# Scores of a pair of heads in two stretches instead of three, with the attention product inside the first

## The chip, the cores and the metric

The kernel runs on one core of a Trainium2 chip. The metric is the device time of one execution in microseconds (us); lower is better. A core has engines that run side by side, each through its own list of instructions in order: TensorE (PE in the profile; its weight loads are PEld), VectorE (DVE), ScalarE (ACT), GpSimd (POOL) and SyncE (SP), which here issues most DMAs. They wait for one another through semaphores. TensorE writes its results to PSUM, which has eight banks of 512 fp32 words per partition; DVE and ACT read them from there.

## The reference

```python
# attention: q, k, v of shape (8, 8, 576, 64), tau = 0.02
scores = scale * np.matmul(q, k.transpose(0, 1, 3, 2))
thresh = np.max(scores, axis=-1, keepdims=True) - tau
scores = np.where(scores >= thresh, scores, -1000000000.0)
scores = scores - np.max(scores, axis=-1, keepdims=True)
attn = np.exp(scores)
attn = attn / (np.sum(attn, axis=-1, keepdims=True) + 1e-09)
attn_out = np.matmul(attn, v)
# bridge: (B, H, S, D) -> (B*S, H*D) = (4608, 512), then the feed-forward block, d_ff = 1536
g = x @ w_gate
silu = g * (1.0 / (1.0 + np.exp(-g)))
out = (silu * (x @ w_val)) @ w_out
```

All is fp32. Each row of scores keeps only what lies within tau of its largest value.

## The kernel before

The eight batches are taken in turn, and in each the eight heads in four pairs. The first four pairs (batch 0) go through an older scheme in the head of the program (up to about 130 us). The other 28 pairs, the "halved" ones, are what the change is about. While their attention runs for batch b, TensorE also computes the feed-forward block of batch b - 1, so that the matmuls of the one fill the time in which the other waits for DVE and ACT. From about 1152 us on, only feed-forward work is left (the tail).

**A pair of heads.** Its 576 queries are cut into nine units of 64. A unit's scores for one head fill 128 partitions x 288 words of PSUM: the partitions hold two groups of 32 queries, each against two halves of the keys. They are made by matmuls on narrow tiles of the array (64 rows x 32 columns), eight of them side by side for two heads. A PSUM bank takes one unit in words 0 to 287; a third unit is laid in the rest of two banks, 144 words in each. So with two banks per head, four in all, a slot of three units (`NU3 = 3`) is computed at once: units 0 and 1 in the banks' first parts, unit 2 in the two halves behind them. A pair has three slots. The other four PSUM banks (`bank0` to `bank3`, handed out by `take`) are for everything else: the attention product and the feed-forward matmuls.

**A slot.** `slot_scores` (L1690) waits until the masks of the slot before have left the banks, takes one tile of two banks per head (`pss`) and issues the matmuls (L1706). `slot_rest` (L1711) then plans, for six score tiles (three units, two heads):

- four reductions on DVE for the negated row maximum (L1727 takes two units of a head, L1729 the third);
- the exchange between the two halves of the keys, on DVE (L1735, L1736) or as four copies on ACT (L1741) and a minimum on DVE (L1745), as `MAX_BY_ACT` says;
- the threshold `th` on ACT (L1748);
- per tile an exponential on ACT (L1752), which reads the scores in PSUM and writes to `pall` in SBUF, and a mask on DVE (L1754), which reads the scores again, zeroes what is below the threshold and sums the row;
- the exchange of the sums on ACT (L1762), total and reciprocal on DVE (L1767, L1768), scaling on ACT (L1780) or POOL (L1777), as `POOLED` says, and a transposition on DVE (L1782).

Which of them waits for which is taken by the framework from the tiles that an instruction reads and writes, in the order in which the program writes the instructions down.

**The attention product** of a pair (`attend`, L1787; matmuls L1803) needs all nine units of it transposed, and takes two of the four general banks. It is issued in the next pair, right ahead of that pair's second slot (L1959), so that product and scores share one visit to the narrow tiles. ACT copies the result to `xall` (L1814, L1815).

**The order.** The program writes its instructions down in an order that a planner works out. A `Job` has an engine, an estimated duration, a rank and its predecessors; `Plan` keeps a clock for each engine and takes the job that can start first, by rank. TensorE's order is fixed by the program: `pe(took, fn, *deps)` first brings all jobs to the clock's time, then writes the matmuls and moves TensorE's clock on. The tables `GV`, `CH`, `CD`, `PLAIN` and `CH0` say how many steps of feed-forward work stand behind each slot. Such a step is one of the seven matmul groups of a `Group` (`pa`, `pb`, `pe`, L994), a nested product of `Deep` (`px`, L1474), a flat one (`py`, L1483), or for the first batches a product of `Outputs` (`po`, L1270) or of a plain group (L1201). A `Group`'s steps wait for copies on ACT (L1001, L1017, L1023, L1038, L1069) and free their banks with DVE (L1047, L1059).

The score matmuls before, and the loop over the slots:

```python
for u, part, keys in ((0, (0, slice(0, SH)), (0, SH)), (1, (1, slice(0, SH)), (0, SH)),
                      (2, (0, slice(SH, SH + SQ)), (0, SQ)), (2, (1, slice(SH, SH + SQ)), (SQ, SH))):
...
for s, (n, x) in enumerate((n, x) for n in range(len(halved)) for x in range(NU3)):
...
    if x == 1 and n > 0:
        prepare_v(seg, attend(halved[n - 1]))
    pss, mark = slot_scores(seg, t)
```

## Time and profile before

| | us |
|---|---|
| runs | 1373.98, 1371.77, 1370.46 |
| median | 1371.77 |
| span of the profiled execution | 1370.5 |

| line | engine, what | times | mean ns |
|---|---|---|---|
| L994 | PE, gate step's matmul, 128x256 | 2496 | 380 to 382 |
| L1706 | PE, score matmul, 288 or 144 wide | 5376 | 345 |
| L1803 | PE, attention product | 4032 | 404 |
| L1752 | ACT, exponential | 504 | 498 |
| L1754 | DVE, mask | 504 | 514 |
| L1727 | DVE, maximum of two units | 168 | 743 |
| L1729 | DVE, maximum of the third unit | 168 | 445 |
| L1762 | ACT, exchange of sums, four to a slot | 336 | 198 |
| L1782 | DVE, transposition | 252 | 765 |
| L1780 | ACT, scaling | 415 | 527 |
| L1777 | POOL, scaling | 89 | 1008 |

The span runs from the first to the last instruction of the profiled execution. Matmuls overlap in the array, so a matmul's duration is not what it costs; the distance from one group's start to the next group's start is. Each fp32 matmul of the program leaves two records in the trace. In a line of the timeline stand the start, the time until the group's last end, engine, line, operation, what is written and read, and how many; a bracket tells how long the engine was idle before and who released it. In the view of waits a line reads: who waited, for whom, then us in total, times, longest.

### The profile page before, as it was taken

What the parts mean: (1) busy time and instruction counts of PE and PEld (TensorE: products, weight loads), DVE (VectorE), ACT (ScalarE), POOL (GpSimd) and SP (SyncE); (2) the same over time, 40 slices, a digit from 0 to 9 for tenths busy, and PEclk for the clock granted to TensorE, in tenths of its full rate; (3) what the DMA queues carried; (4) which work ended last, traced back from release to release, by engine and by line L of the source; (5) the groups of instructions that cost most, each with busy time, mean ns of one, the idle gap of its engine ahead of it and who ended that gap; (6) DMA issues with size and microseconds to landing.
All of it is one profiled execution on the core that took longest, in us unless ns stands there. A gap on an engine that the chain in (4) does not pass through costs nothing.

```text
span 1370.5 us, 39181 instructions
## 1 busy us (share of the span) xinstructions
PE 1352.0 (99%) x15590; PEld 1117.2 (82%) x15590; DVE 1069.8 (78%) x2815; ACT 872.3 (64%) x2261; POOL 717.4 (52%) x665
## 2 busy tenths in 40 slices
PE   8999999999999999999999999999999999999998
PEld 6777787778788788877887888877887788999998
DVE  6788888887877777777778777777777776787786
ACT  6888776666756766676767766776767764330330
POOL 2688598663564669434973387427943593000000
PEclk9999999999999999999999999999999999999999
DMA  8752424545524541554154514553165404524411
GB/s 174 196 191 77 96 60 129 142 122 154 159 52 151 145 99 29 175 165 118 37 169 129 150 36 130 141 145 87 33 195 144 113 19 143 162 77 141 157 64 32
DMA packets 208294, 162.32 MB, mean 118 GB/s; under 512 B 166128, under 2 KB 180464, under 8 KB 202736
## 3 DMA queue, kind: packets, MB, share of 16 engines
q1 hardware_dynamic: 203920, 158.86, 41.1%
q8 instruction: 124, 2.03, 0.7%
q10 hardware_dynamic: 4192, 0.95, 0.3%
q14 instruction: 58, 0.48, 0.1%
HBM read 138.28 MB, written 21.50 MB: 117 GB/s over the span
## 4 chain that ended last, share of the span: by engine, by line
PE 90%; DVE 3%; POOL 2%; SPq 1%; DMA 1%; issue 1%; ACT 1%; ACTq 0%; DVEq 0%; POOLq 0%
PE pb L994 18%; PE pa L994 12%; PE px L1474 12%; PE sc L1706 10%; PE pe L994 9%; PE xa L1803 9%; PE po L1270 5%; PE py L1483 5%; PE sc L1155 2%; PE pg L1201 2%; PE pv L1201 2%; PE pe L1155 1%; SPq L367 1%; POOL big L334 1%; PE sc L1474 1%
## 5 line engine op out<-in xcount | busy, mean ns | idle before, releaser
L1754 DVE SCALAR_TENSOR_TENSOR pall<-sc,th,pall 128x288 f32<-128x288 f32 x504 | 244.0, 514 | 65.6 <-ACT pall L1752 51.2
L994 PE MATMUL pb<-xall,big 128*128 128x256 f32 x1152 | 273.5, 380 | 0.0
L1752 ACT ACTIVATE pall<-sc,nm 128x288 f32<-128x288 f32 x504 | 232.1, 498 | 34.2 <-DVE pall L1754 33.9
L994 PEld LDWEIGHTS pb<-xall,big 128*128 128x128 f32 x1152 | 216.3, 190 | 31.0 <-issue 2.5
L1782 DVE STREAM_TRANSPOSE pall<-pall 128x576 f32<-128x576 f32 x252 | 189.7, 765 | 57.8 <-ACT pall L1780 41.1
L1780 ACT ACTIVATE pall<-pall,ri 128x288 f32<-128x288 f32 x415 | 189.4, 527 | 26.3 <-DVE ri L1768 25.8
L847 POOL TENSOR_TENSOR hall<-hall,tmp 128x512 f32<-128x512 f32 x80 | 102.2, 1277 | 159.0 <-DVE hall L1047 141.6
L994 PE MATMUL pa<-xall,big 128*128 128x256 f32 x768 | 183.4, 382 | 0.0
L994 PEld LDWEIGHTS pa<-xall,big 128*128 128x128 f32 x768 | 143.0, 190 | 22.2 <-issue 2.7
L1706 PE MATMUL sc<-kT,qT 64*32 64x144 f32 (+1 forms) x5376 | 149.7, 345 | 3.0 <-DVE pall L1754 1.7
L1727 DVE TENSOR_REDUCE mx<-sc 128x2 f32<-128x576 f32 x168 | 124.8, 743 | 28.4 <-PE sc L1706 27.9
L1706 PEld LDWEIGHTS sc<-kT,qT 64*32 64x32 f32 x5376 | 98.0, 106 | 56.9 <-issue 21.1
L994 PE MATMUL pe<-xall,big 128*128 128x256 f32 x576 | 137.2, 381 | 0.7 <-issue 0.7
L1803 PE MATMUL xa<-pall,vall 64*32 64x288 f32 x4032 | 132.4, 404 | 0.9 <-DVE hall L1047 0.8
L1777 POOL TENSOR_SCALAR pall<-pall,ri 128x288 f32<-128x288 f32 x89 | 88.7, 1008 | 67.1 <-DVE ri L1768 63.9
L994 PEld LDWEIGHTS pe<-xall,big 128*128 128x128 f32 x576 | 108.5, 190 | 17.5 <-issue 3.0
L1803 PEld LDWEIGHTS xa<-pall,vall 64*32 64x32 f32 x4032 | 76.4, 107 | 50.1 <-issue 7.0
L1762 ACT COPY sums<-sums 32x6 f32<-32x6 f32 x336 | 66.6, 198 | 45.7 <-DVE pall L1754 41.1
L1046 ACT ACTIVATE vall<-tmp 128x512 f32<-128x512 f32 x96 | 60.1, 629 | 24.8 <-POOL tmp L847 9.1
L1483 PE MATMUL py<-wo,hall 128*128 128x256 f32 x336 | 74.8, 379 | 0.0
L1729 DVE TENSOR_REDUCE mx<-sc 128x1 f32<-128x288 f32 x168 | 74.7, 445 | 0.0
L847 POOL TENSOR_TENSOR tmp<-tmp 128x512 f32<-128x512 f32 x36 | 45.8, 1273 | 53.4 <-ACT tmp L1069 53.3
(258 smaller groups left out, 2470.9 us busy)
## 6 DMA issues: line engine op xcount, KB each, us to landing
big<-sums_hbm SPq DMA_DIRECT2D x42, 1024.0 KB, 5.3
big<-sums_hbm SPq DMA_DIRECT2D x48, 768.0 KB, 4.8
vall<-in_v_dram SPq DMA_DIRECT2D x112, 144.0 KB, 3.0
out_dram<-big SPq DMA_DIRECT2D x32, 256.0 KB, 2.9
qT<-in_q_dram SPq DMA_DIRECT2D x112, 72.0 KB, 4.7
kT<-in_k_dram SPq DMA_DIRECT2D x112, 72.0 KB, 3.1
wo<-in_moe_w_gate_dram SPq DMA_DIRECT2D x16, 384.0 KB, 4.5
wo<-in_moe_w_val_dram SPq DMA_DIRECT2D x16, 384.0 KB, 4.6
```

The costliest lines, as they stand in the source:

```text
L847: return lambda: nc.gpsimd.tensor_tensor(out=out, in0=a, in1=b, op=op)
L994: nc.tensor.matmul(ps[:, i], w[:, k_, i * P:(i + 1) * P], x[:, k_, :], start=first and i == k_ == 0, stop=True, skip_group_check=True)
L1474: nc.tensor.matmul(ps, a[:, f, :], ws[n][:, f, :], start=bank_ not in begun, stop=True, skip_group_check=True)
L1483: nc.tensor.matmul(ps(), a[:, f, i * P:(i + 1) * P], operands[o][:, f, :], start=first and f == 0, stop=True, skip_group_check=True)
L1706: nc.tensor.matmul(pss[h][(slice(g * G, (g + 1) * G), *part)], qT[hs, col:col + G], kT[hs, c * SH + keys[0]:c * SH + keys[1]], start=True, ...
L1727: rs.append(job("DVE", 0.72, lambda n=n, tile_=tile_: nc.vector.tensor_reduce(out=mx[:, n:n + 2, 0], in_=tile_[:, :, 0:SH], axis=AX.X, op= ...
L1752: ej = job("ACT", 0.42, lambda x=x, n=n: nc.scalar.activation(ps[x], scs[x], AF.Exp, bias=nm[:, n:n + 1]), ej, *((masks[h, 0], masks[h, 1] ...
L1754: masks[x] = job("DVE", 0.45, lambda x=x, n=n: nc.vector.scalar_tensor_tensor(out=ps[x], in0=scs[x], scalar=th[:, n:n + 1], in1=ps[x], op0 ...
L1777: scaled.append(job("POOL", 1.02, lambda x=x, n=n: nc.gpsimd.tensor_scalar(out=x, in0=x, scalar1=ri[:, n:n + 1], scalar2=None, op0=ALU.mul ...
L1780: scaled.append(job("ACT", 0.46, lambda x=x, n=n: nc.scalar.activation(x, x, AF.Copy, scale=ri[:, n:n + 1]), rj, rank=rank))
L1782: seg["turned"].append(job("DVE", 0.72, lambda both=both: nc.vector.transpose(out=both, in_=both), *scaled, rank=rank))
L1803: nc.tensor.matmul(holds[a].ap()[x * G:(x + 1) * G, 0:SH].rearrange("d (i q) -> d i q", q=G), vr[rs, h, j, ds], p[rs, h, :, j, :], start=( ...
```

## The change

The nine units of a pair are computed in two stretches instead of three slots: a combined one of six units and a plain one of three. In the combined stretch TensorE computes two units (in the banks' first parts, "place 0" and "place 1"), then the attention product of the pair before, then four units: one in the halves behind (`HALVES`), one each in place 0 and place 1 again, and one in two of the general banks (`held`). The first pair keeps three plain stretches.

- The four score banks become one tile, `sc_all`, used throughout; `sc_of` gives each head's half of it, and `sc_users` holds for each place the masks that must have read it.
- `unit_scores` issues one unit; `group_scores` and `group_rest` take the place of `slot_scores` and `slot_rest`, for two, three or four units. Maxima in place 0 or 1 are reduced for both heads of a unit at once, the others head by head. The exchange can be divided between ACT and DVE (`BOTH`).
- The jobs of the first two units go ahead of others (`top=-1`).
- The steps of feed-forward work come from one generator (`sequence`) and new tables (`EARLY`, `SECOND`, `THIRD`, `MAIN`); which scalings go to POOL, who does the exchange, and where weight sums are placed is set anew.
- Smaller ones: `take` may now use the last bank that holds a copied value where it is free 0.8 us sooner; `take_b` and `p1` change which groups copy early; some loads get further predecessors.

```diff
-    ps_s = ctx.enter_context(tc.tile_pool(name="ps_s", bufs=2, space=bass.MemoryType.PSUM))
+    ps_s = ctx.enter_context(tc.tile_pool(name="ps_s", bufs=1, space=bass.MemoryType.PSUM))
...
+    sc_all = ps_s.tile([P, 4, 512], F32, name="sc")
+    sc_of = [sc_all[:, 2 * h:2 * h + 2] for h in range(2)]
...
+    def pieces_of(place, h):
+
+        if place == HALVES:
+            return [(sc_of[h][:, n, SH:SH + SQ], n * SQ, (n + 1) * SQ) for n in range(2)]
+        return [(sc_of[h][:, place, 0:SH] if isinstance(place, int) else place[h].ap()[:, 0:SH], 0, SH)]
...
+    def unit_scores(seg, unit, place, more, *deps):
+
         qT, kT = seg["qT"], seg["kT"]
-        deps, sc_users[:] = sc_users[:], []
-        pss = []
+        held = place if isinstance(place, list) else []
 
         def fn():
-            pss.extend(ps_s.tile([P, 2, 512], F32, name="sc") for _ in heads)
...
+            for pieces in zip(*(pieces_of(place, h) for h in range(2))):
                 for g in range(NG):
                     a, c = divmod(g, 2)
...
+                    for (to, lo, hi), hs in zip(pieces, heads):
+                        col = unit * D + a * G
+                        nc.tensor.matmul(to[g * G:(g + 1) * G], qT[hs, col:col + G], kT[hs, c * SH + lo:c * SH + hi], start=True, stop=True)
+
+        users = [d for x in held for d in x.deps] if held else sc_users.pop(place, [])
+        return pe(UNIT + more, fn, *users, *deps)
...
+        for u in sorted(range(U), key=lambda u: marks[u]):
+            if isinstance(places[u], int):
+                def reduce(u=u):
+                    nc.vector.tensor_reduce(out=both_mx[:, :, u], in_=sc_all[:, places[u]:4:2, 0:SH], axis=AX.X, op=ALU.max, negate=True)
+
+                rs.append(job("DVE", 0.74, reduce, marks[u], rank=top))
+                continue
...
         for h, u in tiles:
             x, n = (h, u), n_of(h, u)
-            ej = job("ACT", 0.42, lambda x=x, n=n: nc.scalar.activation(ps[x], scs[x], AF.Exp, bias=nm[:, n:n + 1]), ej,
-                     *((masks[h, 0], masks[h, 1]) if u == 2 else ()), rank=0)
-            masks[x] = job("DVE", 0.45, lambda x=x, n=n: nc.vector.scalar_tensor_tensor(
+            bank_mates = [masks[h, y] for y in range(U) if (h, y) in masks and HALVES in (places[u], places[y])
+                          and not isinstance(places[y], list) and not isinstance(places[u], list)]
+            ej = job("ACT", 0.44, lambda x=x, n=n: nc.scalar.activation(ps[x], scs[x], AF.Exp, bias=nm[:, n:n + 1]), ej, *bank_mates, rank=top)
+            masks[x] = job("DVE", 0.48, lambda x=x, n=n: nc.vector.scalar_tensor_tensor(
...
+    EARLY = (2, 2, 4, 1, 4, 3, 5, 2, 5)
+    SECOND = (5, 9, 5, 9, 8, 9, 7, 4)
+    THIRD = (5, 9, 6, 8, 10, 7, 2, 3)
+    MAIN = (3, 10, 6, 8, 10, 7, 2, 3)
...
+        if len(units) > 3:
+            marks = group_scores(seg, units[0:2], [0, 1], True, False)
+            group_rest(seg, units[0:2], [0, 1], marks, pooled[0], by[0], 2, top=-1)
             prepare_v(seg, attend(halved[n - 1]))
+            holds = []
+
+            def held():
+                holds.extend(take("sc") for _ in range(2))
+                return holds
+
+            marks = group_scores(seg, units[2:6], [HALVES, 0, 1, held], False, True)
+            group_rest(seg, units[2:6], [HALVES, 0, 1, holds], marks, pooled[1], by[1], 2, BORDER)
+        else:
+            marks = group_scores(seg, units, [0, 1, HALVES], True, True)
```

## The prediction

> **What bounds the kernel now.** First the page's first part, then TensorE's waits.

> ```profile
> span 1370.5 us, 39181 instructions
> PE 1352.0 (99%) x15590; PEld 1117.2 (82%) x15590; DVE 1069.8 (78%) x2815; ACT 872.3 (64%) x2261; POOL 717.4 (52%) x665
> ```
> ```profile
> PE sc L1706 <- DVE pall L1754: 1.7, 2, 1.1
> PE xa L1803 <- DVE hall L1047: 0.8, 5, 0.2
> ```

> TensorE works 99% of the span, and in the attention part its two largest waits are 1.7 and 0.8 us in total. So a microsecond taken from TensorE there counts in full, and so does one that it has to wait. The timeline of TensorE shows what a visit to the scores (L1706) costs:

> ```profile
> 796.43 1.89 PE L994 MATMUL pb<-xall,big 128*128 128x256 f32 x8
> 798.16 1.89 PE L994 MATMUL pa<-xall,big 128*128 128x256 f32 x8
> 799.98 1.72 PE L1706 MATMUL sc<-kT,qT 64*32 64x288 f32 x64
> 801.62 1.99 PE L994 MATMUL pb<-xall,big 128*128 128x256 f32 x8
> 803.45 1.89 PE L994 MATMUL pe<-xall,big 128*128 128x256 f32 x8
> ...
> 783.40 4.60 PE L1803 MATMUL xa<-pall,vall 64*32 64x288 f32 x144
> 787.79 1.70 PE L1706 MATMUL sc<-kT,qT 64*32 64x288 f32 x64
> ```

> A gate step (L994) takes 1.73 us from start to start; before the scores 1.82, after them 1.83. The attention product is 144 records in 4.39 us, eight at a time on the array, so a wave of eight 288-wide ones takes 0.244. A unit is two waves (0.49; one of 144-wide halves is four short waves, the same), three units 1.46, but the visit takes 1.64 inside: a visit costs 0.09 + 0.18 + 0.10 = 0.37 us beside its work.

> Now what hangs on the scores: the reductions (L1727, L1729), the exchange (L1741), the limit (L1748), six exponentials on ACT (L1752), six masks on DVE (L1754), all reading the same PSUM. DVE and ACT in the same slot:

> ```profile
> 801.91 0.72 DVE L1727 TENSOR_REDUCE mx<-sc 128x2 f32<-128x576 f32 x1
> 802.56 0.44 DVE L1729 TENSOR_REDUCE mx<-sc 128x1 f32<-128x288 f32 x1
> ...
> 806.79 0.52 DVE L1754 SCALAR_TENSOR_TENSOR pall<-sc,th,pall 128x288 f32<-128x288 f32 x1 [1.43 <-ACT pall L1752]
> ...
> 807.23 0.52 DVE L1754 SCALAR_TENSOR_TENSOR pall<-sc,th,pall 128x288 f32<-128x288 f32 x1
> ...
> 807.88 0.52 DVE L1754 SCALAR_TENSOR_TENSOR pall<-sc,th,pall 128x288 f32<-128x288 f32 x1
> ```
> ```profile
> 804.06 0.81 ACT L1741 COPY mx<-mx 32x6 f32<-32x6 f32 x4 [0.59 <-DVE mx L1729]
> ...
> 806.06 0.30 ACT L1748 ACTIVATE th<-nm,cut 128x6 f32<-128x6 f32 x1
> 806.27 0.88 ACT L1752 ACTIVATE pall<-sc,nm 128x288 f32<-128x288 f32 x2
> 807.35 0.94 ACT L1752 ACTIVATE pall<-sc,nm 128x288 f32<-128x288 f32 x2 [0.20 <-DVE pall L1754]
> ```

> The third exponential starts at 807.35, 0.04 after the first mask has ended (806.79 + 0.52), though ACT was idle and the two read different banks: accesses of two engines to one PSUM tile go one after the other, in the order written out. Before, each head has its own tile, so the two heads alternate and a mask comes every 0.55 us on average. From these starts: mask to next exponential 0.56, exponential to its mask 0.53.

> **What the change removes.** Visits fall from 85 to 58 (84 score stretches and a last product; now 30 three-unit stretches, 27 combined ones, one product): 27 x 0.37 = 10.0 us gained. The work itself stays: 288-wide score matmuls rise by 216 and 144-wide ones fall by 432, the same time.

> **What it adds: waits in the combined stretch.** All four banks are now one tile (sc_all). In the changed kernel's instruction list each wait names a semaphore's count; in 24 of the 27 combined stretches they read: mask 1 waits for exponential 2, exponential 3 for mask 1, mask 2 for exponential 3, exponential 4 for mask 2, mask 3 for exponential 4; the HALVES unit on TensorE waits for mask 3, mask 4 for HALVES's last matmul, and the unit in place 0 for mask 4. Let T be the first of the two early units' matmuls.
> - Scores end at T + 1.23 (1.72 less two waves). Two reductions of 576: start to start 0.65 (801.91 to 802.56), the last 0.74: T + 2.69 with 0.07 before.
> - Exchange, minimum and limit: 0.81 + 0.13 + 0.2 and hops on ACT, 1.28; on DVE 1.11 (from the slot at 787.79, where reductions end at 791.71 and the first exponential starts at 792.82). First exponential at about T + 3.9.
> - Two exponentials 0.88, then 0.04, 0.56, 0.53, 0.56, 0.53, 0.52 to mask 3's end: T + 7.52; HALVES 0.08 later at T + 7.6.
> - TensorE is there at T + 1.0 + 4.39 = T + 5.39: it waits 2.2. Then HALVES 0.7 with its flight, hop, mask 0.52, hop: place 0 comes 1.35 after HALVES instead of 0.49, another 0.86. Sum 3.07; in the three stretches where both masks precede HALVES, 2.65.
> - 24 x 3.07 + 3 x 2.65 = 81.7 us. Bounds for one stretch: 0.9 if the masks ran at the old pace bank by bank (rival below), 4.0 where the product itself also waits for the last transposes, which now have one stretch less before it. That second wait I worked out for one stretch with eight gate steps before it: transposes and the gate sum end 1.0 to 1.3 late; I take 0.3 on average, 8 us.

> [...]

> **Waits behind it.** The four-unit group's chain is serial too. From place 0: scores of both places end at + 1.2; six reductions 2.8 (four of 0.37 and two of 0.65 apart); exchange and limit 1.25; eight exponentials and masks, of which the shared tile's alternate, end near + 12.4. TensorE has 1.73 and the work up to the next stretch, which by the instruction list and the rows (gate step 1.73, nested product 4.7, flat product 5.2) is 5.2, 10.4, 8.6, 13.8, 18.1, 10.4, 10.3, 17.2 and then, in turn, 9.9, 8.1, 10.3, 17.2 us. Where less than 10.7 there is a wait: 5.5, 0.3, 2.1, 0.3, 0.4 and about 0.8 + 2.6 + 0.4 per block of four pairs. Together some 24 us (0 if gates lag anyway, 40 if foreign instructions stand between). The three-unit chain (+ 11.3) is covered by gaps of 10.3 to 19.3. Gate steps queue behind exponentials on ACT, which is in order: the copies they wait for come 0.4 and 0.2 late in the stretch I walked through, 0.6 in some 13 stretches, 8 us.

> Costed at nothing: 21 scalings move from ACT (0.527) to POOL (1.008), covered by POOL's 48% idle, 21 us if not; loads of q, k and v keep their number and are issued by SP, whose transfers keep 41% of the DMA engines busy; bank choice and late copies add one DVE addition of about 0.7 in all.

> **Sum.** -10.0 + 81.7 + 8 + 24 + 8 = +111.7. 1370.5 + 111.7 = 1482.2 for the span; the median of the runs is 1.3 above the profiled span, so 1483.

> **The rivals.**
> 1. Waits only by bank: the masks keep 0.55 and HALVES waits for its own banks' masks. Mask 4 would end at T + 6.5, HALVES's second half be due at 5.63: 0.9 x 27 = 24, and 5 behind it: 1370.5 - 10 + 24 + 5 + 1.3 = 1391. For it: the earlier kernel waits so little. Against: 807.35, and the waits as listed.
> 2. The other side: faster. By data alone nothing is late: masks 1 and 2 end at T + 5.4 ahead of place 0 at 5.88, mask 4 at 6.5 against place 1 at 6.4. If the product's 4.39 us cover the chain, only the visits count: 1371.8 - 10.0 = 1361.8. It decides if mask 3 ends before T + 5.3; by the rows it does so 2.2 later, and among the 84 stretches of the trace no fourth mask ended sooner than 7.6 after the first score matmul, with one unit more in front.
> 3. The clock drops as TensorE pauses. The granted clock is 0.88 in the first 10 us, where TensorE is busy 6.57, and 1.00 from 785 to 932. If it halved for one visit and one gate step after each combined stretch: 27 x (1.46 + 1.73) = 86 more, 1569. Against: pauses of 2.2 and 0.86 with work between. [...]

> **How the numbers follow.** Forecast 0.83 (own range 1425 to 1525: waits of 2.4 and nothing behind them give 1427, of 4.0 with 45 behind 1515); rival 1 0.06, rival 2 0.07, rival 3 0.04. The range 1385 to 1525 takes in rival 1 and nine tenths of the forecast, 0.81. A measurement of this kernel tells about 0.3% from no change: faster 0.08, same 0.01, slower 0.91.

> **What would show it.** TensorE waiting on the mask line in front of the narrow halves and of place 0, some 2.2 and 0.9 us in each combined stretch, 27 times; exponentials and masks of the early two units in strict turn, 1.1 us a pair; waits on the mask line before three-unit stretches that come 8 to 10 us after a combined one; 58 visits to the narrow tiles. Wrong if HALVES starts right behind the product, or if masks still come every 0.55 us.

## The result and the profile after

The changed kernel takes 1534.58 us (median of 4 runs, 1531.78 to 1539.47) against 1371.12 for the kernel before on the same chip: a ratio of 1.120, with a 95% interval of 1.117 to 1.122. The forecast was 1483 with a range up to 1525: the direction was right, the size too small. The profiled execution has a span of 1529.8 us, 159.3 more than before; the forecast for it was 111.7 more.

From the page of the changed kernel, its first part and two of its costliest groups (busy time and mean ns of one, then the engine's idle time before them and what ended most of it):

```profile
span 1529.8 us, 38164 instructions
...
PE 1379.0 (90%) x15158; PEld 1125.1 (74%) x15158; DVE 1082.3 (71%) x2837; ACT 856.1 (56%) x2214; POOL 744.4 (49%) x691
...
L1806 DVE SCALAR_TENSOR_TENSOR pall<-sc,th,pall 128x288 f32<-128x288 f32 x504 | 248.8, 516 | 206.8 <-ACT pall L1805 180.5
L1805 ACT ACTIVATE pall<-sc,nm 128x288 f32<-128x288 f32 x504 | 230.8, 496 | 117.9 <-DVE pall L1806 114.0
```

The same two groups of the kernel before:

```profile
L1754 DVE SCALAR_TENSOR_TENSOR pall<-sc,th,pall 128x288 f32<-128x288 f32 x504 | 244.0, 514 | 65.6 <-ACT pall L1752 51.2
L1752 ACT ACTIVATE pall<-sc,nm 128x288 f32<-128x288 f32 x504 | 232.1, 498 | 34.2 <-DVE pall L1754 33.9
```

TensorE's share falls from 99% to 90%. A mask still takes 516 ns and an exponential 496; but before its masks DVE now waits 180.5 us for exponentials instead of 51.2, and ACT 114.0 us for masks instead of 33.9. The two engines stand still for one another. TensorE's own waits (for whom, us in total, times, longest):

```profile
PE sc L1732 <- DVE pall L1806: 88.3, 63, 6.3
PE sc L447 <- DVE pall L472: 16.7, 11, 2.5
PE pb L1006 <- ACT tmp L1056: 7.5, 6, 1.4
PE xa L1862 <- DVE pall L1841: 6.1, 5, 2.6
PE pb L1006 <- ACT tmp L1087: 4.7, 13, 0.6
PE sc L453 <- DVE pall L472: 4.2, 4, 1.4
```

Scores waiting for masks: 88.3 us where it was 1.7. The lines L447, L453 and L472 are scores and masks in the head of the program, which the prediction had not looked at. The chain of waits in one combined stretch (start, us, what was being waited out):

```profile
932.61 1.22 PE sc L1732 x32
...
933.85 1.43 DVE mx L1766 x2
...
936.17 0.30 ACT th L1798
...
936.47 0.79 ACT pall L1805 x2
...
937.28 0.54 DVE pall L1806 x2
...
937.84 0.51 ACT pall L1805
...
938.38 0.54 DVE pall L1806 x2
...
938.94 0.51 ACT pall L1805
...
939.47 0.54 DVE pall L1806 x2
...
940.05 0.81 PE sc L1732 x32
...
940.88 0.54 DVE pall L1806 x2
...
941.46 3.07 PE sc L1732 x48
```

This is the prediction's chain almost to the tenth. By the timeline the first of these score matmuls starts at 932.54, so that is the forecast's T. The first exponential starts at T + 3.93 (forecast 3.9), then exponentials and masks come in turn, the halves at T + 7.51 (forecast 7.6), then mask 4, and place 0 comes 1.41 behind the halves (forecast 1.35). The product (by the timeline from 933.53 to 938.1) is not in the chain at all: TensorE then stands still for 1.95 us. What the forecast didn't have is the last line: the 48 matmul records of the last three units in 3.07 us, where the same 48 take 1.69 elsewhere.

By stages, from the spans of four profiled executions (us; "16 pairs" is from the product of the tenth halved pair to that of the 26th; the product stands about a third of a pair earlier in the new order, so some 10 us lie in the last column instead of the second):

| kernel | to the first halved score | to the tenth product | 16 pairs | to the end |
|---|---|---|---|---|
| before | 132.0 | 356.7 | 589.0 | 292.8 |
| changed | 140.8 | 412.0 | 663.6 | 313.3 |
| changed, two tiles (first experiment) | 129.0 | 375.1 | 618.0 | 308.3 |
| before, one tile (second experiment) | 140.7 | 406.2 | 643.2 | 299.2 |

### The profile page after: what moved, and what is told of

It reads as the page before. It is cut to its first block, busy times and chain, and to the rows that moved or that the text cites. A ratio compares the mean times of both kernels' runs of the same rounds, so it can differ in the third digit from the quotient of the medians.

```text
span 1529.8 us, 38164 instructions
## 1 busy us (share of the span) xinstructions
PE 1379.0 (90%) x15158; PEld 1125.1 (74%) x15158; DVE 1082.3 (71%) x2837; ACT 856.1 (56%) x2214; POOL 744.4 (49%) x691
## 3 DMA queue, kind: packets, MB, share of 16 engines
q8 instruction: 120, 1.97, 0.5%
## 4 chain that ended last, share of the span: by engine, by line
PE 41%; DVE 16%; ACT 9%; issue 3%; POOL 1%; DVEq 0%; ACTq 0%; POOLq 0%
PE pb L1006 10%; PE px L1492 8%; PE sc L1732 7%; ACT pall L1805 6%; DVE pall L1806 6%; PE pa L1006 5%; DVE mx L1766 4%; PE py L1501 4%; PE pe L1006 3%; DVE mx L1773 2%; PE sc L1173 1%; DVE pall L1841 1%; ACT mx L1784 1%; PE pe L1173 1%; DVE mx L1779 1%
## 5 line engine op out<-in xcount | busy, mean ns | idle before, releaser
L1806 DVE SCALAR_TENSOR_TENSOR pall<-sc,th,pall 128x288 f32<-128x288 f32 x504 | 248.8, 516 | 206.8 <-ACT pall L1805 180.5
L1805 ACT ACTIVATE pall<-sc,nm 128x288 f32<-128x288 f32 x504 | 230.8, 496 | 117.9 <-DVE pall L1806 114.0
L1006 PE MATMUL pb<-xall,big 128*128 128x256 f32 x1104 | 266.6, 384 | 12.5 <-ACT tmp L1056 7.5
L1006 PEld LDWEIGHTS pb<-xall,big 128*128 128x128 f32 x1104 | 205.9, 191 | 56.2 <-ACT tmp L1056 11.9
L1732 PE MATMUL sc<-kT,qT 64*32 64x288 f32 (+1 forms) x4944 | 164.4, 392 | 88.3 <-DVE pall L1806 88.3
L1836 POOL TENSOR_SCALAR pall<-pall,ri 128x288 f32<-128x288 f32 x110 | 110.5, 1015 | 218.1 <-DVE ri L1827 215.8
L1732 PEld LDWEIGHTS sc<-kT,qT 64*32 64x32 f32 x4944 | 83.5, 112 | 161.2 <-DVE pall L1806 119.8
L1839 ACT ACTIVATE pall<-pall,ri 128x288 f32<-128x288 f32 x394 | 183.1, 527 | 10.1 <-DVE ri L1827 9.2
L1862 PEld LDWEIGHTS xa<-pall,vall 64*32 64x32 f32 x4032 | 99.9, 108 | 38.9 <-DVE tmp L1077 7.2
L1006 PEld LDWEIGHTS pe<-xall,big 128*128 128x128 f32 x576 | 108.6, 190 | 16.6 <-issue 1.4
L1821 ACT COPY sums<-sums 32x4 f32<-32x4 f32 (+2 forms) x336 | 66.7, 199 | 53.3 <-DVE pall L1806 48.9
L1784 ACT COPY mx<-mx 32x6 f32<-32x6 f32 (+2 forms) x162 | 31.7, 196 | 113.7 <-DVE mx L1773 84.6
L1798 ACT ACTIVATE th<-nm,cut 128x6 f32<-128x6 f32 (+2 forms) x84 | 25.0, 297 | 108.6 <-DVE nm L1793 89.7
```

Source lines behind the costliest of these rows:

```text
L1006: nc.tensor.matmul(ps[:, i], w[:, k_, i * P:(i + 1) * P], x[:, k_, :], start=first and i == k_ == 0, stop=True, skip_group_check=True)
L1732: nc.tensor.matmul(to[g * G:(g + 1) * G], qT[hs, col:col + G], kT[hs, c * SH + lo:c * SH + hi], start=True, stop=True)
L1805: ej = job("ACT", 0.44, lambda x=x, n=n: nc.scalar.activation(ps[x], scs[x], AF.Exp, bias=nm[:, n:n + 1]), ej, *bank_mates, rank=top)
L1806: masks[x] = job("DVE", 0.48, lambda x=x, n=n: nc.vector.scalar_tensor_tensor(out=ps[x], in0=scs[x], scalar=th[:, n:n + 1], in1=ps[x], op0 ...
L1836: scaled.append(job("POOL", 1.02, lambda x=x, n=n: nc.gpsimd.tensor_scalar(out=x, in0=x, scalar1=ri[:, n:n + 1], scalar2=None, op0=ALU.mul ...
L1839: scaled.append(job("ACT", 0.46, lambda x=x, n=n: nc.scalar.activation(x, x, AF.Copy, scale=ri[:, n:n + 1]), rj, rank=rank))
```

## The experiments

### One tile per head in the new order, and one tile in the old order

The theory: the shared tile makes accesses of ACT, DVE and TensorE follow one another in the order in which they are written down, and this costs most. The rival: the new order itself is too tight. Each is taken without the other.

```diff
-    sc_all = ps_s.tile([P, 4, 512], F32, name="sc")
-    sc_of = [sc_all[:, 2 * h:2 * h + 2] for h in range(2)]
+    sc_of = [ps_s.tile([P, 2, 512], F32, name=f"sc{h}") for h in range(2)]
...
-                    nc.vector.tensor_reduce(out=both_mx[:, :, u], in_=sc_all[:, places[u]:4:2, 0:SH], axis=AX.X, op=ALU.max, negate=True)
+                            out=mx[:, n:n + 2, 0], in_=sc_of[h][:, :, 0:SH], axis=AX.X, op=ALU.max, negate=True), marks[u], rank=top))
```

> The changed kernel with one PSUM tile of two banks per head instead of one of four banks for both; reductions of the first units per head. Theory (the shared tile puts the exponentials and masks of both heads in strict turn, and that is most of the loss): masks every 0.55 us, TensorE waits under 0.5 us in front of the halves instead of 1.98 (measured in the changed kernel, 53.5 us in 27 stretches); the wait of about 0.9 before place 0 stays, since exponential and mask of head 1's second unit are still written down after the halves; the head of the program gives back 9 us and the waits before the three-unit stretches shrink: 1445 us, 1420 to 1490. Rival (the new order is what is too slow: reductions, exchange and first exponential alone outlast the 4.39 us of the product): over 1510 us.

Measured: 1432.82 us, ratio 1.045 (1.043 to 1.047). So 101.8 of the 163.5 us that the change costs go with the tile. (The 1.98 in this text, and in the text for the step in between, is 2.15: the sum divided there had counted the last product as a stretch too. For the same reason the 8.0 us in the text for "masks first" are 12.4.) DVE in the same kind of stretch:

```profile
780.29 0.52 DVE L1806 SCALAR_TENSOR_TENSOR pall<-sc,th,pall 128x288 f32<-128x288 f32 x1 [0.76 <-ACT pall L1805]
...
780.74 0.52 DVE L1806 SCALAR_TENSOR_TENSOR pall<-sc,th,pall 128x288 f32<-128x288 f32 x1
...
782.29 0.52 DVE L1806 SCALAR_TENSOR_TENSOR pall<-sc,th,pall 128x288 f32<-128x288 f32 x1 [1.03 <-PE sc L1731]
...
783.76 0.52 DVE L1806 SCALAR_TENSOR_TENSOR pall<-sc,th,pall 128x288 f32<-128x288 f32 x1 [0.95 <-PE sc L1731]
```

Masks 1 and 2 (one of each head) come 0.45 apart instead of 1.10, and the halves start at 781.41, between masks 2 and 3. Masks 3 and 4 then wait for the halves and for place 0. On average TensorE waits 0.46 before the halves instead of 2.15.

The other half of the pair: the kernel before, whose four score banks are made one tile.

```diff
-    ps_s = ctx.enter_context(tc.tile_pool(name="ps_s", bufs=2, space=bass.MemoryType.PSUM))
+    ps_s = ctx.enter_context(tc.tile_pool(name="ps_s", bufs=1, space=bass.MemoryType.PSUM))
...
+    sc_all = ps_s.tile([P, 4, 512], F32, name="sc")
+    sc_of = [sc_all[:, 2 * h:2 * h + 2] for h in range(2)]
...
-            pss.extend(ps_s.tile([P, 2, 512], F32, name="sc") for _ in heads)
+            pss.extend(sc_of)
```

> The kernel before with its four score banks as one tile and nothing else changed, so the old order with the changed kernel's tile. Theory (tile): the span from the first exponential of a slot to its last mask grows from 4.3 us (median) by 1.9, against a median slack of 1.97 to the next scores: about 44 us of waits, and 9 in the head of the program, 1424 us, 1395 to 1450. Rival (one tile costs only where the new order puts TensorE right behind the masks): under 1385 us.

Measured: 1490.52 us, ratio 1.086 (1.084 to 1.088): 119.3 us lost without any change of order, more than twice what I expected. The timelines of DVE and of ACT in one slot show the mechanism:

```profile
790.46 0.52 DVE L1762 SCALAR_TENSOR_TENSOR pall<-sc,th,pall 128x288 f32<-128x288 f32 x1 [1.15 <-ACT pall L1760]
...
790.90 0.51 DVE L1762 SCALAR_TENSOR_TENSOR pall<-sc,th,pall 128x288 f32<-128x288 f32 x1
...
792.39 0.52 DVE L1762 SCALAR_TENSOR_TENSOR pall<-sc,th,pall 128x288 f32<-128x288 f32 x1 [0.96 <-ACT pall L1760]
```
```profile
789.55 0.87 ACT L1760 ACTIVATE pall<-sc,nm 128x288 f32<-128x288 f32 x2
...
791.46 0.90 ACT L1760 ACTIVATE pall<-sc,nm 128x288 f32<-128x288 f32 x2 [0.18 <-DVE pall L1762]
793.39 0.89 ACT L1760 ACTIVATE pall<-sc,nm 128x288 f32<-128x288 f32 x2 [1.03 <-DVE pall L1762]
```

Two exponentials, two masks, two exponentials: the engines never work on scores at the same time, and a pair takes 1.93 us where it took 1.09 in the slot of the prediction (806.79 to 807.88). From the first exponential's start to the last mask's end a slot now takes 6.1 us (median of 84) instead of 4.3: 1.8 more, and 1.9 were expected. TensorE's waits show what I had left out:

```profile
PE sc L1714 <- DVE pall L1762: 58.8, 39, 4.4
PE pb L1002 <- ACT tmp L1046: 17.9, 10, 2.5
```

The 58.8 us on scores are near the 44 expected. The copies that gate steps need are queued on ACT behind exponentials that wait for masks (17.9). The granted clock is 0.989 instead of 0.997: 32.0 us of TensorE's busy time lie in stretches at 0.50, against 6.7 in the kernel before. If work at 0.50 takes twice its time (the 48 records above took 3.07 us instead of 1.69), half of the difference is lost, 13 us. This is an estimate from the clock's records and the matmuls of the two traces; no run separates it.

The two together: the tile costs 119 us in the old order and 102 in the new one; the order costs 62 us with two tiles and 44 with one. The tile is the larger part, and the order costs too. The tile's part holds what the clock loses behind its waits: 51.3 us of TensorE's busy time lie at 0.50 in the changed kernel and 6.8 with two tiles, by the same estimate 22 of the 102 us.

### The head of the program

Only the head gets a tile per turn again; the two-stretch part keeps the shared one.

```diff
-    sc_all = ps_s.tile([P, 4, 512], F32, name="sc")
...
+    head_pools = ExitStack()
+    ps_h = head_pools.enter_context(tc.tile_pool(name="ps_h", bufs=2, space=bass.MemoryType.PSUM))
+
+    def next_sc():
+        return ps_h.tile([P, 2, 512], F32, name="sc")
...
+    head_pools.close()
+    ps_s = ctx.enter_context(tc.tile_pool(name="ps_s", bufs=1, space=bass.MemoryType.PSUM))
+    sc_all = ps_s.tile([P, 4, 512], F32, name="sc")
```

> The changed kernel with one tile for both heads in the two-stretch part, but a tile of two banks for each turn in the head of the program, as before. Theory (the shared tile alone makes the first score matmul of the two-stretch part late, 140.8 us against 132.0, through waits of 16.7 and 4.2 us for the head's masks): 1534.6 - 8.8 = 1526 us, 1520 to 1530. Rival (the head is late for another reason, or its lateness is made good later): 1534 within 4.

Measured: 1525.56 us. The 9.0 us are there and stay to the end.

### Is the wait slack, and does the clock matter?

Every product but the last issues its first step three times more: 1.46 us of TensorE work put right where the wait is, with nothing that could depend on it.

```diff
-            for j in range(NK):
+            again = 3 if i < len(halved) + NP - 1 else 0
+            for n_, j in enumerate([0] * again + [*range(NK)]):
...
-                                         vr[rs, h, j, ds], p[rs, h, :, j, :], start=(j == 0), stop=(j == NK - 1))
+                                         vr[rs, h, j, ds], p[rs, h, :, j, :], start=(j == 0), stop=(j == NK - 1 or n_ < again))
```

> The changed kernel with the first of the nine steps of every attention product but the last issued three times more (48 matmuls of 64x288, each pass starts afresh, so the sums are the same): 6 waves of 0.244, 1.46 us more TensorE work between the early units and the halves, 27 times 1.46 = 39.5 us. Theory (the halves wait for mask 3, whose time the product does not set): the halves start when they did, the work fits into the wait of 1.98 us, and no time is added; where the clock fell to 0.50 behind the wait it now stays at 1.00, which by the stretches seen at half pace is worth 0 to 20 us: 1518 us, 1510 to 1537. Rival (the clock drop costs nothing): 1534 within 4. Rival (the wait hangs on the product): 1574.

Measured: 1525.77 us, ratio 1.112 (1.109 to 1.115), 8.8 us less than without the extra work, though 39 us of work were added. The stretch that answers to the one above:

```profile
931.16 6.03 PE L1863 MATMUL xa<-pall,vall 64*32 64x288 f32 x192
937.67 0.73 PE L1732 MATMUL sc<-kT,qT 64*32 64x144 f32 x32 [0.49 <-DVE pall L1806]
939.09 1.69 PE L1732 MATMUL sc<-kT,qT 64*32 64x288 f32 x48 [0.69 <-DVE pall L1806]
```

From the product's start to the halves it takes 6.51 us, as in the changed kernel (933.53 to 940.05: 6.52). So the wait does not hang on the product, and what was put into it is free. And the 48 records take 1.69 again instead of 3.07. They do so in all 27 stretches; in the changed kernel eight of the 27 took 2.51 to 3.14.

With both side costs taken away:

> The edits of e9_head_two_tiles and e5_fill together: the head of the program gets its own tiles back, and every product but the last issues its first step three times more, so that TensorE pauses less ahead of the halves. Two costs that the prediction had at nothing are taken away: the late head (9.0 us when alone taken away) and the clock at 0.50 behind the waits (8.8). Theory (they are separate): they add up, 1534.6 - 17.8 = 1517 us, 1511 to 1522. Rival (the early start of the two-stretch part is used up by the same waits, or the clock falls elsewhere instead): 1524 or more.

Measured: 1513.99 us. They add up; the 3 us more are about what two such medians differ by.

### A step between the product and the last four units

```diff
             prepare_v(seg, attend(halved[n - 1]))
+            next(seq)
             holds = []
...
-        for _ in range(table[kk]):
+        for _ in range(table[kk] - (len(units) > 3)):
             next(seq)
```

> The changed kernel, one tile, with one feed-forward step (1.73 us where it is a gate step) taken from behind the combined stretch and put between the attention product and the last four units. Theory (the four units only wait for masks that end at a time of their own): the step fills the wait of 1.98 us, the wait between halves and place 0 goes, since mask 4 is now written down ahead of the halves; minus 46, minus 11 to 22, minus up to 15 for a clock that no longer drops, plus 10 for 27 more visits, plus 14 before the three-unit stretches, whose gap gets shorter: 1485 us, 1450 to 1510. Rival (the wait is tied to the end of the product, not to the early units' masks): 1534 or more.

Measured: 1586.74 us, 52 slower than the changed kernel, where I expected 50 faster. TensorE in one stretch, and three of its waits:

```profile
703.64 2.20 PE L1732 MATMUL sc<-kT,qT 64*32 64x144 f32 x80 [0.67 <-DVE pall L1806]
...
711.14 1.97 PE L1006 MATMUL pe<-xall,big 128*128 128x256 f32 x8 [1.65 <-DVE pall L1806]
```
```profile
PE py L1501 <- DVE pall L1806: 26.6, 5, 5.3
...
PE pe L1006 <- DVE pall L1806: 17.1, 12, 1.7
PE pa L1006 <- issue: 16.0, 4, 5.3
```

What the step was meant to do it did: the four units run in one go and wait 0.67 at their start. But gate steps and flat products now wait for masks. By the changed list of instructions they wait for the mask of the held unit: the step in between takes one general bank, the step behind the stretch gets a bank that the held unit's scores are still in, and the planner had reckoned with these masks earlier than they come.

The same edit with two tiles:

> Two tiles, and one feed-forward step between the attention product and the last four units (the edits of e1_two_tiles and e3_step_between together). What is left of the loss with two tiles (1432.8 - 1371.3 = 61.5 us) lies by the theory mostly in the combined stretch: from the product's start to the work behind the stretch it takes 8.39 us (median) where the work alone is 4.39 + 4 x 0.49 + 0.1 = 6.45, 52 us in 27 stretches, since the product covers only 4.39 of the early units' chain. The step covers 1.73 more and takes these 52 away, against 10 for 27 more visits. But with one tile the steps behind the stretch then waited for the held unit's masks (26.6 + 17.1 us, and 16 for an addition queued behind masks), because the banks had been given to it: with masks twice as dense I expect half of that, 30 us. 1432.8 - 52 + 10 + 30 = 1421 us, 1400 to 1445. Rival (the rest is not the cover but the banks and the short gaps): 1445 or more, with no wait left in the stretch.

Measured: 1513.93 us, ratio 1.103 (1.100 to 1.106), 81 slower than with two tiles alone. This rival held. One stretch of it:

```profile
823.48 4.63 PE L1862 MATMUL xa<-pall,vall 64*32 64x288 f32 x144
828.04 1.99 PE L1005 MATMUL pb<-xall,big 128*128 128x256 f32 x8
829.96 2.20 PE L1731 MATMUL sc<-kT,qT 64*32 64x144 f32 x80
```

No wait is left in this stretch (and 6.48 from the product to the halves is 4.39 + 1.73 + 0.36: the price of a visit, forecast as 0.37). Behind it the waits for banks are as large as with one tile (26.5, 19.5 and 18.1 us for the three lines of the list above). The clock falls behind these waits too: the granted clock is 0.968 against 0.998 with two tiles alone, and 78.4 us of TensorE's busy time lie at 0.50 against 6.8, by the estimate above some 36 of the 81 us. So this experiment doesn't say what the cover of the early units alone is worth: it put a dearer wait in its place.

### Masks written down ahead of the halves, and the held unit first

Two further edits on the two-tile kernel, since it still waited around the halves. The first makes the halves wait for all early masks in the planner's clock:

```diff
         users = [d for x in held for d in x.deps] if held else sc_users.pop(place, [])
+        if place == HALVES:
+            users = users + sc_users.get(0, []) + sc_users.get(1, [])
```

> The kernel with one tile per head, and the halves now also wait, in the planner's clock, for all four masks of the early units, so that these are written down ahead of the halves. With two tiles TensorE still waited 0.3 us before the halves and then 0.8 and 0.5 between the halves and places 0 and 1 (8.0 and about 30 us in all), because exponential 4 and mask 3 or 4 were written down behind the halves' matmuls. Theory (those waits come from the order of writing down): the halves wait about 1.1 for mask 4, then nothing: 0.8 less in each of 27 stretches, 1432.8 - 21 = 1411 us, 1398 to 1424. Rival (the waits are the chain's own length, whoever is written first): 1430 or more.

Measured: 1440.76 us, 8 slower. From the product's start to the work behind the stretch it now takes 7.73 us (median) instead of 8.39: 0.66 less, near the 0.8 expected. But once in four pairs this stands in TensorE's timeline, and in DVE's:

```profile
914.89 3.60 PE L1005 MATMUL pa<-xall,big 128*128 128x256 f32 x8 [4.53 <-issue]
```
```profile
913.50 0.52 DVE L1808 SCALAR_TENSOR_TENSOR pall<-sc,th,pall 128x288 f32<-128x288 f32 x1 [0.76 <-ACT pall L1807]
...
914.38 0.41 DVE L859 TENSOR_TENSOR big<-big,px 128x256 f32<-128x256 f32 x1
```

The gate step waits 4.53 us. The view of waits names nobody ("issue"); by the list of instructions it waits for the addition at 914.38, which empties a bank of the nested product and is queued on DVE behind masks that wait for exponentials. The step then runs at half pace (3.60 instead of 1.97). The four such waits of the trace add up to 18.1 us, about what 27 times 0.66 had gained, and the half pace comes on top. So the wait went and a rarer, longer one came.

The same with one tile:

> The changed kernel, one tile, with the same edit: the halves wait for all four early masks. Theory: mask 4 ends 0.53 behind mask 3, so the halves start 0.53 later, and place 0 follows without the 0.9 that it waited in 23 stretches: 1534.6 - 10 = 1525 us, 1516 to 1533. With the shared tile the wait is thus moved, not removed; if it fell by more than 20, the order of writing down and not the tile would be the larger cause.

Measured: 1532.61 us; the difference to 1534.58 is within the runs' spread. With the shared tile the wait is only moved.

Then two tiles, the masks first, and the held unit as the first behind the product:

```diff
-            marks = group_scores(seg, units[2:6], [HALVES, 0, 1, held], False, True)
-            group_rest(seg, units[2:6], [HALVES, 0, 1, holds], marks, pooled[1], by[1], 2, BORDER)
+            marks = group_scores(seg, units[2:6], [held, HALVES, 0, 1], False, True)
+            group_rest(seg, units[2:6], [holds, HALVES, 0, 1], marks, pooled[1], by[1], 2, BORDER)
```

> Two tiles, all early masks ahead of the halves, and the unit in general banks moved from fourth to first behind the product: it needs no mask, only two free banks. If the banks were free at once it would cover 0.49 of the 1.1 us that the halves wait: 1398 us. But by the list of instructions it waits in many stretches for the copies of the product's own two banks on ACT (0.65 us each and a hop): then it starts about 1.2 behind the product and covers nothing: 1411. I expect 1408, 1392 to 1425.

Measured: 1426.16 us, ratio 1.039 (1.035 to 1.042), the fastest of the new order and one microsecond above the range I gave. The unit waits for the copy of the product out of its bank, as the list said:

```profile
929.93 4.63 PE L1864 MATMUL xa<-pall,vall 64*32 64x288 f32 x144
935.45 2.57 PE L1731 MATMUL sc<-kT,qT 64*32 64x288 f32 x80 [0.88 <-ACT xlast L1876]
```

No version tried is faster than the kernel before.

## Why the prediction was right and wrong

The mechanism was right. What failed is the sum: it had nothing for the shared tile in the head of the program (9.0 us) and nothing for a clock that falls behind the waits (8.8), and its terms for late copies and for the product were too small (10 and 4 us).

- **The reason was right.** "All four banks are now one tile", and so the engines take turns: the tile alone is worth 102 us in the new order and 119 in the old. Rival 1 (waits bank by bank, 1391) and rival 2 (faster) fall with it. By the row at 780.74 of the first experiment, DVE's mask 2 reads head 1's tile until 781.26, while ACT's third exponential, on head 0's, starts at 780.86: with a tile per head the two engines read scores at the same time. What took turns was the program's order within one tile.
- **Waits in the combined stretch** (forecast 81.7): the halves start 2.15 later than the product alone would let them (start to start, less 4.39, mean of 27; forecast 2.2), and place 0 another 0.9 in 24 stretches (forecast 0.86 in 24). That makes 58 + 22 = 80. Right.
- **Visits** (forecast -10.0): the trace has the 58 visits, and one costs 0.36 by the row at 829.96, forecast 0.37. No run removes visits alone.
- **Waits before three-unit stretches** (forecast 24): adding up TensorE's idle times before and within them gives 23.5. Right in sum, but by luck: the first pairs, up to 366 us, gave 16.6 where the forecast had 8.6 (two waits of 6.35 and 4.76 among them), and the blocks of four pairs behind gave 6.9 where it had about 15.
- **The product waits for transposes and the gate sum** (forecast 8): the time from the early units' start to the product is 12 over the 1.0 it should be, 27 stretches together. Somewhat too small.
- **Gate steps behind exponentials** (forecast 8): the waits for copies on ACT add up to 17.6 (7.5 and 4.7 in the list above, and two lines below it with 3.2 and 2.2). The forecast was less than half of it.
- **The head of the program, at nothing: wrong.** `sc_all` is "used throughout", as the text on the change says, but the sum only followed it into the combined stretches. 9.0 us.
- **The clock, at nothing: wrong.** Rival 3 was set aside with "Against: pauses of 2.2 and 0.86 with work between"; that the clock stays up through such pauses no run had shown. In eight of the 27 stretches the work behind these pauses ran at half pace; filling the pause took that away in all eight and gave 8.8 us back. The rival's size (86 us) was wrong too, since it had all 27 stretches at half pace.
- **The range** ended at 1525, built from larger waits alone; the two terms at nothing were not in it. With both taken away the kernel runs at 1514, which the range would have held. Of the 47.6 us between forecast and span, the head takes 8.8, the slower last units of the stretches about 12 (the time from the halves to the work behind, less four units and the waits at place 0), the copies 10 and the product 4, against 2 forecast too much for the stretch. Some 15 us are left. Slower matmuls outside these places are among them (the granted clock is 0.90 to 0.93 from 200 to 300 us): by the estimate used above, work at a clock of 0.50 loses some 7 us between 166 and 289 us, behind the waits of 6.35 and 4.76 above all, and 2 right behind the stretches. That wasn't tried by a run, and the last 6 us stay open.
- **Scalings, loads, bank choice, at nothing**: none of the waits listed names them.

That the order itself loses 62 us with two tiles is measured; that this is the early units' chain being longer than its cover is shown only in part. From the product's start to the work behind the stretch it takes 8.39 us where the work is 6.45, 52 us in 27 stretches, but every edit that shortened this brought up another wait.

## What to carry to other kernels

When buffers are merged into one tile, list every reader and writer that is now ordered, in all parts of the program, and not only in the part that the merge was made for. A wait that is removed by moving work uses up something else, here a bank or a place in DVE's queue: look at who gets that bank next before you count the gain. A pause on TensorE costs more than its length where the clock falls behind it: here the 48 records behind such pauses took up to 3.14 us instead of 1.69. Before the fall at 725.90 of the changed kernel stand two pauses, of 1.64 and 0.68 us, with TensorE busy for 1.09 of the last 3.41 us; so look at TensorE's busy share over some microseconds and not at the longest pause alone. Filling a pause with work that costs nothing else is a cheap way to see both the slack and the clock (here 39 us of work went in, and the kernel took 8.8 us less).

## What the hardware showed that I had not expected

TensorE at half pace after pauses of 2 us: 3.07 us instead of 1.69 for the same 48 matmul records. Two stretches of the changed kernel, first their score matmuls in the timeline, then two windows for each stretch, cut at whole multiples of 3.413 us from the clock's fall at 940.94 (a window's length, the busy time of PE, PEld, DVE, ACT and POOL, then the granted clock, DMA share and GB/s):

```profile
940.05 0.72 PE L1732 MATMUL sc<-kT,qT 64*32 64x144 f32 x32 [1.95 <-DVE pall L1806]
941.46 3.07 PE L1732 MATMUL sc<-kT,qT 64*32 64x288 f32 x48 [0.69 <-DVE pall L1806]
...
1019.83 0.73 PE L1732 MATMUL sc<-kT,qT 64*32 64x144 f32 x32 [2.16 <-DVE pall L1806]
1021.24 1.69 PE L1732 MATMUL sc<-kT,qT 64*32 64x288 f32 x48 [0.69 <-DVE pall L1806]
```
```profile
937.52:940.94 3.41, 1.30 (x56) 0.47 (x39) 1.39 (x7) 1.72 (x6) 2.72 (x3) 1.00 0.27 68
940.94:944.35 3.41, 2.89 (x48) 1.11 (x48) 1.08 (x4) 0.78 (x4) 3.40 (x5) 0.50 0.97 197
...
1016.03:1019.44 3.41, 1.64 (x56) 1.00 (x40) 1.24 (x5) 2.22 (x7) 1.25 (x1) 1.00 0.22 54
1019.44:1022.86 3.42, 2.35 (x80) 1.25 (x81) 1.17 (x5) 1.27 (x8) 0.00 (x0) 1.00 1.17 201
```
